# Chunk 1's triangular inverse on VectorE, behind chunk 0's, with none on GpSimd

## The chip, the cores and the metric

The kernel runs on one core of a Trainium2 chip. The metric is the device time of one execution in microseconds, the median of three runs. The engines of the core are TensorE (PE: matmuls, and PEld: loads of their stationary side), VectorE (DVE), ScalarE (ACT), GpSimd (POOL) and SyncE (SP, which issues most DMAs).

## What is computed

A delta-rule attention over 768 steps for 4 x 8 heads of width 48, then a dense layer pair with silu, then a mixture of 8 experts with top-1 routing.

```python
k_n = k / (np.linalg.norm(k, axis=-1, keepdims=True) + 1e-06)
for t in range(S):
    y[:, :, t] = np.einsum('bhd,bhde->bhe', q[:, :, t], state)
    v_old = np.einsum('bhde,bhd->bhe', state, kt)
    state = state + bt[:, :, :, None] * np.einsum('bhd,bhe->bhde', kt, vt - v_old)
h = x @ w_in;  x = (h * (1.0 / (1.0 + np.exp(-h)))) @ w_out      # 3072 x 384, inner 2048
out = x.copy(); out[do_compute] = xc + gate * (relu(xc @ w1[e]) @ w2[e])
```

## The kernel before

**Chunks.** The 768 steps are cut into 12 chunks of 64. In a chunk the recurrence becomes a triangular system for each of the 32 heads: `grams` makes the products of keys (tiles `g`, then `Gd` and `G21`), `inverse(c)` inverts the 32x32 diagonal blocks of all heads at once into the tile `Xb`, and `chain(c, b)` uses `Xb` for each of the four batches b: `ks`, `u1`, `g21u`, `u2` (tiles `ru`, `vp`, `U`, `SU`), the new state (`supd`, tile `St`) and the output of the chunk (`yout`, tiles `py` and `x`; a high part and a rest, `lo`). When the last `lo` of a chunk is there, two DMAs `x<-x` finish the tile, and the dense layers of that chunk can start: `l1(c, m)` (matmuls `hp<-x,w`) and `l2(c, m)` (`xp<-gh,w` and `xp<-gl,w`) for 16 blocks m. `x2out` then takes the sum `xp` out (`xt`), and transposes it for the router (matmuls `xr`, tile `xs`).

**The inverse.** It transposes `Gd` into `Gi`, makes the norms in 18 small instructions (tile `nw`), and then goes through 31 columns j from 31 to 1 with two instructions each, `mul` (writes `tmp`) and `sub` (writes `X`). Each depends on the one before it. `last()` scales `X` and transposes it into `Xb`. Chunk 0 works in `X`/`Gi0`; chunk 1 works in `X1` (a part of the tile `spare`) and in `Gi1`, two tiles that lie where the dense weights of blocks 13 and 14 go later, so the loads of those (`raw` of `late`) wait for chunk 1's inverse.

**Where chunk 1's inverse runs.** `E = nc.gpsimd if c == 1 else V` (line 487): all 62 column instructions of chunk 1, and two scalings of `Gi` ahead of them, are GpSimd's; the transposes, the norms and `last` are VectorE's.

**The weights.** The dense weights come as 64-bit floats. `convert` turns each of 32 blocks into a pair of fp32r tiles: ScalarE scales the high words (`w<-raw`), VectorE does one shift (TENSOR_SCALAR) and two merges (SCALAR_TENSOR_TENSOR `w<-raw,w`), ScalarE copies the high part, and GpSimd, or VectorE for 8 of the 32, subtracts it for the rest (TENSOR_TENSOR `w<-w,w`). This goes on while chunk 0's and chunk 1's chains and chunk 0's dense layers run.

**The order.** Up to chunk 1's chain the order on each engine is made when the kernel is built, by a scheduler that goes by priorities (`rank`: CHAIN, PREP, INV, CONV, MOE of a chunk) and by its own estimate of times. From chunk 2 on `period(c)` writes the order out by hand. Each engine works through its instructions strictly in that order.

Of the kernel before, what the change touches and what calls it, by code (L numbers as in the profile page):

```python
# [57 lines left out]
def kernel(  # L58
# [25 lines left out]
    nc = InOrder(tc)  # L84
# [352 lines left out]
    def inverse(c):  # L437

        steps = []
        V = nc.vector  # L440
# [43 lines left out]
        steps.append(lambda: V.tensor_tensor(out=w[4], in0=w[3], in1=bet[:, c, :], op=ALU.mult))  # L484
        steps.append(lambda: V.tensor_tensor(out=w[4], in0=w[4], in1=w[3], op=ALU.mult))

        E = nc.gpsimd if c == 1 else V
        pre = E is nc.gpsimd

        def scale(y0):  # L490
            return (nc.gpsimd if c else V).tensor_tensor(
# [4 lines left out]
        def flat(j, r0, r1):  # L496
            f = (r0 - j // 2) * j
            return tmp[:, f:f + (r1 - r0) * j].rearrange("p (n j) -> p n j", j=j)

        def mul(j, r0, r1):  # L500
# [3 lines left out]
            if pre:  # L504
                return E.tensor_tensor(out=flat(j, r0, r1), in0=a, in1=b, op=ALU.mult)
            return V.scalar_tensor_tensor(
# [3 lines left out]
        def sub(j, r0, r1):  # L510
            return E.tensor_tensor(
                out=X[:, r0:r1, 0:j], in0=X[:, r0:r1, 0:j], in1=flat(j, r0, r1), op=ALU.subtract
            )
# [565 lines left out]
    def prep():  # L1079
        while free and todo:  # L1080
            g = todo.popleft()
            c, b = g // B, g % B
            j = slots[g] = free.popleft()
            with rank(c - 1, PREP):
                if c == 0 and b == B - 1:
                    prep_0()
                elif c:
                    with rank(c - 2, PREP) if c > 1 else rank(-2, 3):
                        if c == 1:
                            clear(j)  # L1090
                            load_kt(c, b, j, nc.sync)
                        load_qk(c, b, nc.sync)
                        nc.sync.dma_start(out=PQ[j], in_=qp[c, b])
                    if c > 1:
                        prep_t(c, b)
                        if c == FIRST:
                            prep_g(c, b)
                    elif b == B - 1:
                        js1[:] = [slot(c, i) for i in range(B)]
                        grams(c, js1, 1)  # L1100
            if b == B - 1 and 0 < c < FIRST:
                with rank(0, INV):
                    last_of[c] = inverse(c)
            if b == B - 1 and not c:
                return
# [45 lines left out]
    def period(c):  # L1151


        more = c + 2 < NCH
        late = LATE if c == FIRST else 0
        inv = deque(inverse(c + 1) if c + 1 < NCH else ())
        if late:
            inv.extendleft(reversed(inverse(c)))
# [306 lines left out]
```

## Time and profile before

| what | value |
|---|---|
| median of three runs | 906.33 us (905.14 to 906.43) |
| the profiled execution | 903.69 us |
| its span, first to last instruction | 902.0 us |
| PE busy | 811.0 us, 90% |
| DVE busy | 618.6 us, 69% |
| ACT busy | 474.8 us, 53% |
| POOL busy | 367.3 us, 41% |
| mean granted clock of TensorE | 0.935 of full speed |

Times in the rows are microseconds from the span's start. The rows show one execution, the profiled one. A row of the timeline is: start, duration, engine, line, operation, what it writes `<-` what it reads, shape, how many merged; in brackets the idle time of the engine before it and what ended that. All instructions of the kernel's own work carry line 43, that of the helper that records them, so one goes by tile names.

### The profile page before, as it was taken

What the parts mean: (1) busy time and instruction counts of PE and PEld (TensorE: products, weight loads), DVE (VectorE), ACT (ScalarE), POOL (GpSimd) and SP (SyncE); (2) the same over time, 40 slices, a digit from 0 to 9 for tenths busy, and PEclk for the clock granted to TensorE, in tenths of its full rate; (3) what the DMA queues carried; (4) which work ended last, traced back from release to release, by engine and by line L of the source; (5) the groups of instructions that cost most, each with busy time, mean ns of one, the idle gap of its engine ahead of it and who ended that gap; (6) DMA issues with size and microseconds to landing.
All of it is one profiled execution on the core that took longest, in us unless ns stands there. A gap on an engine that the chain in (4) does not pass through costs nothing. (4 is left out here: it accounts for less than half of the span.)

```text
span 902.0 us, 26074 instructions
## 1 busy us (share of the span) xinstructions
PE 811.0 (90%) x10385; PEld 775.4 (86%) x10385; DVE 618.6 (69%) x1776; ACT 474.8 (53%) x1290; POOL 367.3 (41%) x533
## 2 busy tenths in 40 slices
PE   9075987797899999999999999999998968999994
PEld 9074977786799999999999999999998968999994
DVE  4998795698586877778697777779424029765731
ACT  3257875336465564746566574744455354555620
POOL 5477553151333433333342333334345452454320
PEclk7565899899899999999999999999999989999998
DMA  8963211212421414133221414211109126767300
GB/s 291 400 223 109 68 40 40 49 38 60 131 76 48 123 52 142 52 98 96 58 88 52 142 51 125 70 46 33 42 4 299 27 59 198 246 215 222 105 21 24
DMA packets 66355, 96.10 MB, mean 107 GB/s; under 512 B 10730, under 2 KB 47672, under 8 KB 66224
## 3 DMA queue, kind: packets, MB, share of 16 engines
q1 hardware_dynamic: 63408, 89.70, 32.7%
q0 software_dynamic: 2816, 4.65, 1.8%
q8 instruction: 83, 1.36, 0.7%
q14 instruction: 48, 0.39, 0.2%
HBM read 80.79 MB, written 12.91 MB: 104 GB/s over the span
## 5 line engine op out<-in xcount | busy, mean ns | idle before, releaser
L43 POOL TENSOR_TENSOR gl<-gf,gh 128x256 fp32r<-128x256 f32 x192 | 149.1, 777 | 348.2 <-ACT gf L43 304.1
L43 PE MATMUL hp<-x,w 128*128 128x256 f32 x1728 | 256.0, 293 | 8.9 <-DMA x<-x 3.9
L43 PEld LDWEIGHTS hp<-x,w 128*128 128x128 f32 x1728 | 224.2, 194 | 17.0 <-DVE xs L43 5.2
L43 PE MATMUL xp<-gh,w 128*128 128x256 f32 x1152 | 172.6, 286 | 6.9 <-ACT gh L43 6.4
L43 PEld LDWEIGHTS xp<-gh,w 128*128 128x128 f32 x1152 | 153.9, 192 | 8.1 <-ACT gh L43 7.1
L43 DVE SCALAR_TENSOR_TENSOR tmp<-X,nw,Gi 128x126 f32<-128x126 f32 (+22 forms) x341 | 139.0, 408 | 10.4
L43 ACT ACTIVATE gh<-hp 128x256 fp32r<-128x256 f32 x192 | 73.7, 384 | 135.2 <-PE hp L43 134.3
L43 DVE TENSOR_TENSOR X<-X,tmp 128x126 f32<-128x126 f32 (+22 forms) x341 | 101.9, 299 | 8.6
L43 PE MATMUL xp<-gl,w 128*128 128x256 f32 x576 | 103.5, 288 | 2.1 <-POOL gl L43 2.0
L43 PEld LDWEIGHTS xp<-gl,w 128*128 128x128 f32 x576 | 82.8, 191 | 4.2 <-POOL gl L43 3.1
L43 ACT ACTIVATE gf<-hp 128x256 f32<-128x256 f32 x192 | 72.6, 378 | 5.7 <-POOL gl L43 5.6
L43 PE MATMUL ehp<-exh,ew 128*128 128x256 f32 x384 | 66.5, 282 | 0.0
L43 ACT ACTIVATE SU<-St 32x192 f32<-32x192 f32 (+1 forms) x176 | 63.6, 361 | 2.7
L43 DVE COPY_PREDICATED PQ<-mU,g 128x512 f32<-128x512 uint8 x44 | 32.3, 738 | 46.6 <-ACT G L43 40.8
L43 ACT ACTIVATE ew<-eraw 128x768 fp32r<-128x768 f32 x64 | 53.3, 843 | 20.7 <-PE yp L43 14.8
L43 PE MATMUL g<-kq,KtB 128*128 128x128 f32 (+1 forms) x384 | 54.3, 299 | 9.8 <-DVE PQ L43 6.4
L43 DVE TENSOR_TENSOR vp<-vp,ru 64x192 f32<-64x192 f32 x92 | 31.6, 347 | 45.3 <-PE ru L43 41.4
L43 DVE TENSOR_TENSOR ew<-eraw,ew 128x768 fp32r<-128x768 f32 x48 | 49.9, 1046 | 17.7 <-ACT ew L43 17.5
L43 PEld LDWEIGHTS g<-kq,KtB 128*128 128x128 f32 x384 | 50.9, 212 | 11.0 <-DVE PQ L43 6.9
L43 PEld LDWEIGHTS ehp<-exh,ew 128*128 128x128 f32 x384 | 58.3, 190 | 0.0
L43 PE MATMUL yp<-ew,egh 128*128 128x384 f32 x256 | 57.5, 341 | 0.0
L43 POOL TENSOR_TENSOR ew<-eraw,ew 128x768 fp32r<-128x768 f32 x16 | 30.3, 1895 | 57.4 <-ACT ew L43 57.2
(144 smaller groups left out, 1276.6 us busy)
## 6 DMA issues: line engine op xcount, KB each, us to landing
eraw<-in_w_dram SPq DMA_DIRECT2D x64, 384.0 KB, 4.4
kq<-in_qk_dram SPq DMA_DIRECT2D x44, 256.0 KB, 3.9
PQ<-in_qp_dram SPq DMA_DIRECT2D x44, 256.0 KB, 4.3
ki<-in_ki_dram SPq DMA_DIRECT2D x44, 192.0 KB, 2.9
raw<-in_w_out_dram SPq DMA_DIRECT2D x16, 384.0 KB, 7.0
raw<-in_w_in_dram SPq DMA_DIRECT2D x16, 384.0 KB, 7.8
x2s<-xs SPq DMA_DIRECT2D x48, 98.5 KB, 2.3
v<-in_v_dram SPq DMA_DIRECT2D x24, 192.0 KB, 3.9
```

The lines of the kernel that those rows point to most:

```text
L43: r = f(*args, **kw)
```

## The change

Line 487 becomes `E, pre = V, False`. Chunk 1's inverse then takes the branch of the other chunks: `mul` is one SCALAR_TENSOR_TENSOR on VectorE that multiplies by the scale `w[4]` on its way, `sub` a TENSOR_TENSOR on VectorE, and the two scalings of `Gi1` fall away.

```diff
-        E = nc.gpsimd if c == 1 else V
-        pre = E is nc.gpsimd
+        E, pre = V, False
```

The scheduler then builds another order for everything up to chunk 1's chain. Three places of it follow. Names are as in the kernel; a number behind a name is its buffer: `X_122`, `tmp_126`, `Gi_121` are chunk 0's inverse, `spare`, `tmp_127`, `Gi_123` and `Gi_124` chunk 1's, `w_...` weights, which got other numbers.

VectorE, in the middle of chunk 0's inverse (column 14 and on), before:

```order
L43 SCALAR_TENSOR_TENSOR tmp_126<-X_122,nw,Gi_121 128x126
L43 TENSOR_TENSOR X_122<-X_122,tmp_126 128x9x14
L43 SCALAR_TENSOR_TENSOR tmp_126<-X_122,nw,Gi_121 128x130
L43 TENSOR_TENSOR X_122<-X_122,tmp_126 128x10x13
L43 SCALAR_TENSOR_TENSOR tmp_126<-X_122,nw,Gi_121 128x120
```

VectorE at the same place, after:

```order
L43 SCALAR_TENSOR_TENSOR tmp_126<-X_122,nw,Gi_121 128x126
L43 SCALAR_TENSOR_TENSOR tmp_127<-spare,nw,Gi_124 128x31
L43 TENSOR_TENSOR X_122<-X_122,tmp_126 128x9x14
L43 TENSOR_TENSOR spare<-spare,tmp_127 128x31
L43 SCALAR_TENSOR_TENSOR tmp_126<-X_122,nw,Gi_121 128x130
L43 SCALAR_TENSOR_TENSOR tmp_127<-spare,nw,Gi_124 128x30
L43 TENSOR_TENSOR X_122<-X_122,tmp_126 128x10x13
L43 TENSOR_TENSOR spare<-spare,tmp_127 128x30
```

From here to the end of chunk 0's inverse, 29 instructions of chunk 1's stand between chunk 0's; the other 33 stand one by one among the conversions behind it.

VectorE, where chunk 1's inverse ends (`Xb<-spare`), before:

```order
L43 SCALAR_TENSOR_TENSOR w_1019<-raw_272,w_1019 128x384
L43 TENSOR_TENSOR w_1024<-w_1019,w_1024 128x384
L43 TENSOR_TENSOR spare<-spare,nw 128x512
L43 TENSOR_SCALAR w_1034<-w_1034 128x384 x2
L43 STREAM_TRANSPOSE Xb<-spare 128x32x16
```

VectorE, the same place, after:

```order
L43 TENSOR_TENSOR spare<-spare,tmp_127 128x16
L43 SCALAR_TENSOR_TENSOR nw<-nw 128x32
L43 TENSOR_TENSOR spare<-spare,nw 128x512
L43 TENSOR_SCALAR w_1122<-w_1122 128x384
L43 TENSOR_TENSOR nw<-nw 128x32
L43 TENSOR_TENSOR w_1112<-w_1107,w_1112 128x384
L43 STREAM_TRANSPOSE Xb<-spare 128x32x16
```

`w_1024` of before is the `l2` weight of block 8, `w_1112` of after that of block 14 (the `w_1114` of before): `Xb` of chunk 1, and with it chunk 1's chain, now stands behind most of the conversions.

TensorE, where chunk 0's dense layers end and chunk 1's begin, before:

```order
L43 MATMUL xp<-gh,w_1114 128x256 x6
L43 MATMUL hp<-x,w_971 128x256 x7
L43 MATMUL xp<-gl,w_1114 128x256 x3
L43 MATMUL hp<-x,w_971 128x256 x2
L43 MATMUL xp<-gh,w_1129 128x256 x6
L43 MATMUL xp<-gl,w_1129 128x256 x3
L43 MATMUL xr<-iwg,xt 128x138 x6
L43 MATMUL hp<-x,w_986 128x256 x9
```

TensorE, the same place, after:

```order
L43 MATMUL xp<-gl,w_1127 128x256 x3
L43 MATMUL py<-PQ_115,SU_118 64x64
L43 MATMUL ru<-SU_118,ki 48x48 x8
L43 MATMUL py<-PQ_115,SU_118 64x64 x7
L43 MATMUL ru<-SU_119,ki 48x48 x8
L43 MATMUL py<-PQ_116,SU_119 64x64 x8
L43 MATMUL hp<-x,w_969 128x256 x9
L43 MATMUL xr<-iwg,xt 128x138 x6
L43 MATMUL hp<-x,w_984 128x256 x9
```

The end of chunk 1's chain (`py`) now stands behind the last matmul of chunk 0's dense layers, and nothing stands between it and chunk 1's first `hp`.

## Rows read from the trace of the kernel before

**Rows 1.** Busy us of each engine, granted clock (PEclk), DMA share, GB/s, by stage.

```profile
core 0: us, PE busy (x) PEld busy (x) DVE busy (x) ACT busy (x) POOL busy (x), PEclk, DMA share, GB/s
51.00:82.50 31.50, 22.40 (x437) 20.29 (x435) 31.02 (x61) 23.50 (x59) 27.11 (x41) 0.61 0.47 142
147.86:190.90 43.04, 32.46 (x294) 31.00 (x294) 28.91 (x92) 15.16 (x47) 11.52 (x15) 0.92 0.18 35
190.90:902.00 711.10, 673.61 (x8806) 646.12 (x8806) 469.26 (x1395) 375.73 (x1023) 264.61 (x366) 0.98 0.33 96
50.04:123.45 73.41, 58.82 (x892) 54.36 (x890) 63.07 (x122) 55.95 (x147) 50.49 (x68) 0.70 0.32 99
```

**Rows 2.** GpSimd: chunk 1's inverse begins; its busy us from 51 on.

```profile
35.48 2.16 POOL L43 TENSOR_TENSOR Gi<-Gi,nw 128x512 f32<-128x512 f32 x2 [5.84 <-DVE nw L43]
...
51.00:86.40 35.40, 21.75 (x39) 0.60 0.43 128
```

**Rows 3.** VectorE's timeline: undisturbed conversions, chunk 1's Xb, a weight's rest.

```profile
77.38 0.35 DVE L43 TENSOR_SCALAR w<-w 128x384 int32<-128x384 int32 x1
77.65 0.54 DVE L43 SCALAR_TENSOR_TENSOR w<-raw,w 128x384 int32<-128x384 int32 x1
...
86.31 0.69 DVE L43 TENSOR_TENSOR spare<-spare,nw 128x512 f32<-128x512 f32 x1 [3.83 <-POOL spare L43]
...
87.45 1.05 DVE L43 STREAM_TRANSPOSE Xb<-spare 128x512 f32<-128x512 f32 x1
...
122.26 0.36 DVE L43 TENSOR_TENSOR vp<-vp,ru 64x192 f32<-64x192 f32 x1 [1.31 <-PE ru L43]
...
123.45 1.15 DVE L43 TENSOR_TENSOR w<-w,w 128x384 fp32r<-128x384 f32 x1
```

**Rows 4.** VectorE: the last lo of chunks 0, 1, 2, and chunk 2's Xb.

```profile
78.39 0.41 DVE L43 TENSOR_TENSOR x<-py,x 128x256 fp32r<-128x256 f32 x1
...
143.86 0.42 DVE L43 TENSOR_TENSOR x<-py,x 128x256 fp32r<-128x256 f32 x1
...
186.83 1.13 DVE L43 STREAM_TRANSPOSE Xb<-X 128x512 f32<-128x512 f32 x1
...
222.15 0.41 DVE L43 TENSOR_TENSOR x<-py,x 128x256 fp32r<-128x256 f32 x1
```

**Rows 5.** TensorE: the first hp of chunks 0 and 1, the second xr.

```profile
82.50 4.18 PE L43 MATMUL hp<-x,w 128*128 128x256 f32 x18 [1.58 <-DMA x<-x]
...
147.86 1.07 PE L43 MATMUL hp<-x,w 128*128 128x256 f32 x7 [0.72 <-DMA x<-x]
...
154.72 0.97 PE L43 MATMUL xr<-iwg,xt 128*128 128x138 f32 x6 [2.36 <-ACT gf L43]
```

**Rows 6.** VectorE's timeline, the same inverse beside GpSimd's, and its end.

```profile
45.20 0.43 DVE L43 TENSOR_TENSOR X<-X,tmp 128x70 f32<-128x70 f32 x1
...
50.04 1.05 DVE L43 STREAM_TRANSPOSE Xb<-X 128x512 f32<-128x512 f32 x1
```

**Rows 7.** VectorE's timeline, chunk 0's inverse with the norms (nw) in between.

```profile
31.08 0.36 DVE L43 SCALAR_TENSOR_TENSOR tmp<-X,nw,Gi 128x133 f32<-128x133 f32 x1
31.35 0.19 DVE L43 SCALAR_TENSOR_TENSOR nw<-nw 128x32 f32<-128x32 f32 x1
31.47 0.30 DVE L43 TENSOR_TENSOR X<-X,tmp 128x133 f32<-128x133 f32 x1
31.69 0.18 DVE L43 SCALAR_TENSOR_TENSOR nw<-nw 128x32 f32<-128x32 f32 x1
```

**Rows 8.** Groups of VectorE, 50 to 82.4 us: xcount, busy us, mean ns.

```profile
L43 DVE SCALAR_TENSOR_TENSOR w<-raw,w 128x384 int32<-128x384 int32 x23 | 14.9, 679 | 0.0
L43 DVE TENSOR_SCALAR w<-w 128x384 int32<-128x384 int32 x11 | 5.6, 529 | 0.2 <-ACT w L43 0.2
```

**Rows 9.** ScalarE's timeline around the second xr.

```profile
151.04 2.96 ACT L43 ACTIVATE SU<-St 32x192 f32<-32x192 f32 x8
...
154.29 0.38 ACT L43 ACTIVATE gf<-hp 128x256 f32<-128x256 f32 x1
```

## The prediction

> **What bounds the kernel now.** I read the page first, then a table of busy time by stage, then the timelines of the engines from 30 to 230 us, and last the order that the change gives. From 190.90 us to the end TensorE is busy 673.6 of 711.1 us [rows 1], and the order there is written by hand and stays. So what the change does is done before that point, and it reaches the end one to one: a start of chunk 2's chain that comes 1 us earlier ends the kernel 1 us earlier.
>
> Before it, three things follow each other. From 51 to 82.5 us (chunk 0's chain beside the weight conversions) VectorE is busy 31.02 of 31.50 us: it is the bound, and TensorE and ScalarE are not [rows 1]. GpSimd works on chunk 1's inverse from 35.48 us on, and VectorE stands idle 3.83 us for it until 86.31 [rows 2, 3]. Then chunk 0's dense layers go as the conversions let them, with chunk 1's chain between them, until chunk 1's x is there: its last `lo` ends at 144.28, and its first `hp` starts at 147.86, having waited 0.72 us for the DMA `x<-x` [rows 4, 5]. From 147.86 to 190.90 TensorE works 32.46 of 43.04 us [rows 1]; chunk 2's inverse on VectorE sets the pace, and its loop can go on only when the second `xr` (154.72) has been taken out. So I follow the second `xr`: where it lands, the rest lands.
>
> **What the change adds, removes and moves.** The sum goes along VectorE up to `Xb` of chunk 1, then along the chain.
>
> Chunk 0's `Xb`: it starts at 50.04 [rows 6]. After the change the stretch from 35.3 on holds 27 instructions of chunk 0's inverse and 29 of chunk 1's, in turn. Two chains in turn hide each other's latency: where norms stand between, the next instruction starts 0.27 us after a product of 133 elements, 0.22 after a subtraction of 133 and 0.12 after one of 32 [rows 7]. With sizes from 16 to 136 I take 0.20 as the mean: 56 x 0.20 = 11.2. Three conversion steps (a shift takes 0.27 from start to start, a merge, 0.54 long, some 0.47) [rows 3] and the scaling (0.69 long [rows 3], some 0.6) make 13.0: 35.6 + 13.0 = 48.6, 1.4 us earlier. That one chain took 14.7 us before is GpSimd's doing: beside it a subtraction of 70 elements lasted 0.43 us, one of 133 alone 0.30 [rows 6, 7]. If the two chains did not overlap at all it would be 52 to 54, 2 to 4 later.
>
> Chunk 1's `Xb`: in the new order it stands right behind the rest of `l2`'s block 14, which in the trace comes at 123.45. From 50.04 to there VectorE was busy 63.07 of 73.41 us [rows 1, 3]. To these 73.4 us come the other 33 instructions of the inverse, 33 x 0.20 = 6.7. Off go nine instructions of chunk 1's chain, now behind (`vp` is 0.36 long, `x` 0.41, less what overlaps: 0.3 each, 2.6) [rows 3, 4], the wait of 3.83 for GpSimd and one of 1.31 for that chain [rows 3]. And off goes what GpSimd's inverse took from VectorE. Undisturbed, a merge lasts 0.54 us and a shift 0.35 [rows 3]; from 50 to 82.4 their means were 0.679 and 0.529 [rows 8], so 23 x 0.14 + 11 x 0.18 = 5.2 us were lost beside 27.1 us of GpSimd work [rows 1], 0.19 per us. The column instructions lost a little more [rows 6], and I take 0.25: of 21.75 us of GpSimd's inverse [rows 2] 5.4 us. Together 73.4 + 6.7 - 2.6 - 5.1 - 5.4 = 67.0, less 0.4 since `Xb` (1.05 long, some 0.9) now comes behind that place and the rest (some 0.5) in front of it: 48.6 + 66.6 = 115 us, against 87.45 [rows 3]. The loss per us of GpSimd could be 0 (its other work moves up and collides in its place) or 0.4: 121 or 112.
>
> Chunk 1's chain: from `Xb` to the end of the last `lo` chunk 0 took 50.04 to 78.80, 28.8 us, with all four batches side by side; chunk 2, in two halves with dense blocks between, took 186.83 to 222.56, 35.7 us [rows 4, 6]. Chunk 1's own 87.45 to 144.28 [rows 3, 4] is no guide: over fifty conversion instructions of VectorE stood between, and now seventeen do. It goes in two halves like chunk 2, but with fewer dense blocks between, so 31, with 28.8 and 35.7 as ends: the last `lo` ends at 146 (140.8 to 157).
>
> From there: 3.6 us for the DMA (78.80 to 82.50 and 144.28 to 147.86) [rows 4, 5], so the first `hp` is at 149.6, 1.8 us later than before; 1.4 to 2.1 us for the nine matmuls (seven took 1.07 at 147.86, eighteen 4.18 at 82.50) [rows 5], and 0.9 for `gh` and `gf` (0.38 each [rows 9]), which free the buffer of the second `xr`. It would start at 152.3. Before, it started at 154.72, since ScalarE first made eight copies `SU<-St` of 2.96 us and then `gh` and `gf` [rows 5, 9]; in the new order these copies stand ahead, between the `x` of the chain. So the late `hp` is more than paid for: 152.3 - 154.72 = **-2.4 us**.
>
> The rest costs nothing that I can find. GpSimd loses 30 us of work and nobody waits for what is left. The load of block 13's weights waits for the last product of the inverse, some 3 us ahead of `Xb`, and is wanted about 7 us later. The conversions end some 13 us behind chunk 1's `Xb`, by 130, and chunk 0's last dense block needs them until about 140: in front of the chain's end at 146.
>
> The profiled execution has 902.0 us from first to last instruction and 903.69 in all, 2.64 less than the median of 906.33. The difference of -2.4 goes on the median: **903.9 us**.
>
> **A rule against the change.** From 51 to 82.5 us VectorE has 0.48 us to spare and gets more work [rows 1]. The Trainium skill (Perfetto Trace Analysis, Optimizing Scalar/DVE Operations) says that with VectorE saturated work may be moved to ScalarE or even GpSimd, though it warns that VectorE and GpSimd share a read port. By the first half this change goes the wrong way, and `Xb` of chunk 1 would be at 121; by the warning most of what is added comes back.
>
> **The rivals.**
>
> *Slower: chunk 1's chain comes too late behind the conversions.* Break-even is a last `lo` at 148.4: `Xb` at 115 and a chain of 33.4, or a chain of 31 and `Xb` at 117.4. For it: VectorE was full, ScalarE works 56 of 73.4 us in the same stretch [rows 1] and must turn every conversion round, and chunk 2's chain took 35.7 us. With 117 and 35.7 the second `xr` is at 159, +4.3: 910.6 us; with 121 it is +8, 914.6. Against it: the relief that the rows show.
>
> *No change.* The copies that kept `gf` at ScalarE come back at the same place in another form (the copies now stand between the last two `x`, and can delay the last `lo` by 2 to 3 us instead), or a chain of 33 us: within 1.8 us of 906.3. That the change does not do what it says is excluded by the order: no column instruction is left on GpSimd.
>
> *Much faster: a GpSimd instruction stops VectorE for as long as it lasts.* With 0.5 us lost per us of GpSimd, twice what I take, the relief is 10.9 instead of 5.4, and the second `xr` is 5.5 earlier still: 898.4 us. The rows say 0.19 to 0.25, so it has little weight. This is what the Trainium skill (SBUF — State Buffer, Who interferes with whom) makes likely: a VectorE instruction with two SBUF inputs contends with a GpSimd one that reads SBUF, and whoever issues first holds the port pair for the whole instruction. The trace agrees in kind (merges of 0.679 against 0.54 us), not in full size.
>
> **How the numbers follow.** Chances: forecast (gain of 1.8 to 6 us) 0.41, much faster 0.06, no change 0.25, slower 0.28. A measurement of this kernel can tell about 0.2%, 1.8 us, from no change: faster 0.47, same 0.25, slower 0.28. The range takes in the much faster case down to 899.5 and the slower one up to 911; left out are the ends where 121 and 35.7, or 112 and 28.8, come together.
>
> **What would show it.** Right: VectorE's steps between 36 and 48 us of 0.2 us and `Xb` at 48 to 49; chunk 1's `Xb` at 112 to 119 without a wait for GpSimd; merges from 50 to 82 us nearer to 0.54; the first `hp` of chunk 1 at 148 to 151 after an idle TensorE of 5 us, and the second `xr` about 2 us behind it. Wrong: merges as slow as before; a last `lo` later than 148.4; waits of VectorE for ScalarE's `w` that add up to more than 5 us from 50 to 115; TensorE's granted clock staying near the 0.61 of 51 to 82.5 us [rows 1] while chunk 1's chain runs, so that each matmul step of the chain is longer.

## The result: slower by 1.1%

The kernel after takes 916.23 us (median of 4 runs, 914.65 to 917.9), the kernel before on the same chip 906.38 (4 runs, 905.14 to 906.82): a ratio of 1.0113 with a 95% interval of 1.0095 to 1.0132. The forecast was 903.9 us, the range 899.5 to 911. What came is the prediction's rival "Slower: chunk 1's chain comes too late behind the conversions", at its far corner (914.6 us there).

The head of the page of the kernel after, and under it VectorE's timeline of the places of [rows 3, 4, 6]:

```profile
span 914.9 us, 26069 instructions
...
PE 814.0 (89%) x10385; PEld 778.4 (85%) x10385; DVE 622.1 (68%) x1838; ACT 474.3 (52%) x1290; POOL 339.9 (37%) x469
```

```profile
49.42 1.05 DVE L43 STREAM_TRANSPOSE Xb<-X 128x512 f32<-128x512 f32 x1
...
122.39 1.12 DVE L43 STREAM_TRANSPOSE Xb<-spare 128x512 f32<-128x512 f32 x1
...
149.53 0.63 DVE L43 TENSOR_TENSOR vp<-vp,ru 64x192 f32<-64x192 f32 x2 [6.08 <-PE ru L43]
...
156.66 0.42 DVE L43 TENSOR_TENSOR x<-py,x 128x256 fp32r<-128x256 f32 x1 [1.63 <-ACT x L43]
165.21 0.19 DVE L43 TENSOR_REDUCE xs<-xr 128x10 f32<-128x30 f32 x1 [8.12 <-ACT xs L43]
```

VectorE works only 3.5 us more than before (622.1 against 618.6 us), and nobody works much longer. What has changed is when things happen. Chunk 0's `Xb` comes at 49.42 (forecast 48.6, before 50.04), chunk 1's at 122.39 instead of 87.45, and chunk 1's last `lo` ends at 157.1 instead of 144.3. VectorE has nothing to do for 8.12 us after that. TensorE's timeline, to be held against [rows 5], says why:

```profile
161.01 2.26 PE L43 MATMUL hp<-x,w 128*128 128x256 f32 x9 [5.15 <-DMA x<-x]
163.07 2.49 PE L43 MATMUL xr<-iwg,xt 128*128 128x138 f32 x12
```

TensorE itself stands still for 5.15 us until chunk 1's `x` is complete. The second `xr` (the seventh of these twelve) starts at 164.45, 9.7 us later than before [rows 5]; the median is 9.85 us later. So the delay of that point did reach the end one to one, as the prediction had it, only with the other sign.

The table of busy time by stage (columns as in [rows 1]), for the kernel after:

```profile
36.00:50.00 14.00, 3.35 (x32) 3.32 (x33) 14.00 (x62) 1.51 (x3) 1.08 (x1) 0.50 1.03 402
50.00:82.40 32.40, 21.67 (x443) 19.74 (x441) 31.94 (x72) 23.92 (x62) 10.10 (x10) 0.66 0.51 157
82.40:122.40 40.00, 29.71 (x197) 27.60 (x197) 37.41 (x79) 25.12 (x65) 23.23 (x21) 0.88 0.11 30
49.42:122.40 72.98, 51.96 (x643) 47.92 (x642) 69.92 (x151) 49.03 (x127) 33.33 (x30) 0.78 0.30 90
```

and for the kernel before, in the same stretches:

```profile
50.00:82.40 32.40, 23.40 (x446) 21.27 (x444) 31.90 (x62) 23.50 (x59) 27.01 (x41) 0.61 0.49 150
82.40:122.40 40.00, 34.41 (x437) 32.09 (x438) 30.16 (x60) 31.75 (x87) 22.44 (x26) 0.76 0.20 61
```

Only up to 82.4 us does GpSimd (the fifth engine of a row) have less to do, 10.10 us instead of 27.01. From there to chunk 1's `Xb` it works as long as before, 23.23 against 22.44 us, while VectorE goes from 30.16 to 37.41. TensorE loses 4.7 us of work in that second stretch: chunk 1's chain, which stood between chunk 0's dense blocks, is missing there and comes later; some five to seven of chunk 0's dense blocks are still there beside it, and beside its last 4.6 us (from 152.48) none.

### The profile page after: what moved, and what is told of

Its sections match the earlier page's. It is cut to its first block, busy times and chain, and to the rows that moved or that the text cites. A ratio compares the mean times of both kernels' runs of the same rounds, so it can differ in the third digit from the quotient of the medians.

```text
span 914.9 us, 26069 instructions
## 1 busy us (share of the span) xinstructions
PE 814.0 (89%) x10385; PEld 778.4 (85%) x10385; DVE 622.1 (68%) x1838; ACT 474.3 (52%) x1290; POOL 339.9 (37%) x469
## 5 line engine op out<-in xcount | busy, mean ns | idle before, releaser
L43 PE MATMUL hp<-x,w 128*128 128x256 f32 x1728 | 258.0, 294 | 18.2 <-DMA x<-x 7.2
L43 DVE SCALAR_TENSOR_TENSOR tmp<-X,nw,Gi 128x126 f32<-128x126 f32 (+22 forms) x341 | 135.3, 397 | 10.0
L43 PE MATMUL ehp<-exh,ew 128*128 128x256 f32 x384 | 66.6, 283 | 0.0
L43 ACT ACTIVATE ew<-eraw 128x768 fp32r<-128x768 f32 x64 | 53.3, 843 | 20.4 <-PE yp L43 14.7
```

Of the source, the lines that this page charges most:

```text
L43: r = f(*args, **kw)
```

## The experiments

Theory **place**: the loss is that chunk 1's `Xb` stands behind nearly all conversions, so that its chain ends after everything else. Theory **load**: the 62 added instructions cost VectorE these 10 us wherever they stand. Beside it stands the question where the relief went that the prediction expected of GpSimd. Each time is to be held against the runs of the kernel before on its own chip, so ratios are given.

**e1: the same work, another place.** Each conversion step is tied to one more of the last 33 instructions of chunk 1's inverse, and what is left to the last of them.

```diff
-            with tc.issue_after(gates.popleft() if gates else done):
+            with tc.issue_after(gates.popleft() if gates else tail):
...
+    n = 0.0
+    for i in pace["inv", 1][48:]:
+        n += 1.0
+        while n >= 1:
+            gates.append(i.ins)
+            n -= 1
+    tail = pace["inv", 1][-1].ins
```

> The kernel after, with each conversion step of VectorE behind the second one tied to one more of the last 33 column instructions of chunk 1's inverse, so that the inverse gets every second place on VectorE instead of every third or fourth; the work is the same. In the new order chunk 1's Xb has 43 rows fewer in front of it (row 245 instead of 288). Theory 'place' (the loss of 9.9 us comes from chunk 1's Xb standing behind nearly all conversions, 122.4 us instead of 87.5, so that its chain ends after everything else): Xb of chunk 1 at 92 to 100 us, the last lo of chunk 1 back at 143 to 149, time 904 to 909 us. Theory 'load' (VectorE is full up to that point and the 62 added column instructions cost their 10 us wherever they stand): the conversions end 8 to 10 us later than in the kernel before, chunk 0's last dense block and chunk 1's chain with them, time 913 to 917 us.

Measured: 906.96 us (10 runs) against 905.4 (22 runs), ratio 1.002, 1.0003 to 1.0037. VectorE's and TensorE's timelines:

```profile
88.99 1.12 DVE L43 STREAM_TRANSPOSE Xb<-spare 128x512 f32<-128x512 f32 x1
...
133.90 0.41 DVE L43 TENSOR_TENSOR x<-py,x 128x256 fp32r<-128x256 f32 x1
...
138.65 1.95 DVE L43 SCALAR_TENSOR_TENSOR w<-raw,w 128x384 int32<-128x384 int32 x4
```

```profile
152.92 0.97 PE L43 MATMUL xr<-iwg,xt 128*128 128x138 f32 x6 [2.36 <-ACT gf L43]
```

All columns are still VectorE's, yet eight of the ten microseconds are back. `Xb` is at 88.99, the last `lo` ends at 134.3, ten microseconds ahead of the kernel before, and the conversions end behind it, at 140.6. The second `xr` is held by ScalarE as in [rows 5, 9]. `Xb` and `lo` came earlier than place had expected, but its time was hit. The ten microseconds at the `lo` brought nothing, because another path is now the later one: chunk 0's last dense matmul ends at 148.79 (before 150.59), and the second `xr` starts 4.1 us behind that in both.

**e5: the same place, without the work.** The kernel before, with GpSimd's inverse; only the last three instructions of it wait.

```diff
+            seen["rest", m, z] = (nc.vector if z and m % 2 == 0 else nc.gpsimd).tensor_tensor(
...
-    with rank(0, INV):
+    with rank(0, INV), tc.issue_after(seen["rest", 14, 1].ins):
         last_of.pop(1)()
```

> The kernel before, GpSimd's inverse and all, with one wait more: the last three instructions of chunk 1's inverse (nat, the scaling and Xb) wait for VectorE's rest of l2's block 14, the instruction behind which they stand in the kernel after. VectorE gets no instruction more than in the kernel before. Theory 'place': the loss comes back without the added work; Xb of chunk 1 at 112 to 122 us, the last lo 33 to 36 us behind it, time 909 to 916 us. Theory 'load' (62 more instructions on VectorE make the loss): 905 to 907 us.

Measured: 914.12 us (4 runs) against 905.65 (17 runs), ratio 1.0082, 1.0056 to 1.0108. VectorE's timeline, its waits from 82.4 to 123 us (us in total, times, the longest), the busy time there, and TensorE's timeline:

```profile
122.98 1.07 DVE L43 STREAM_TRANSPOSE Xb<-spare 128x512 f32<-128x512 f32 x1
...
155.00 0.42 DVE L43 TENSOR_TENSOR x<-py,x 128x256 fp32r<-128x256 f32 x1 [1.63 <-ACT x L43]
```

```profile
DVE w L43 <- ACT w L43: 6.5, 3, 4.5
DVE PQ L43 <- ACT G L43: 3.0, 1, 3.0
```

```profile
82.40:122.40 40.00, 31.55 (x213) 29.42 (x213) 30.78 (x58) 26.49 (x69) 26.56 (x30) 0.84 0.12 37
```

```profile
158.93 2.26 PE L43 MATMUL hp<-x,w 128*128 128x256 f32 x9 [4.73 <-DMA x<-x]
160.99 2.76 PE L43 MATMUL xr<-iwg,xt 128*128 128x138 f32 x12
```

`Xb` is a microsecond later than place had expected and the last `lo` follows it by 32.4 us (33 to 36 expected), but the time was hit. VectorE is idle for 9.2 of these 40 us, and the kernel is slow all the same; the end has the shape of the kernel after, with TensorE 4.73 us idle in front of the first `hp`. e1 and e5 together settle it: **the place makes the loss** (0.82% by it alone), and the added work a small part (0.2% in e1, 0.37% by the upper end of its interval; 0.3% between e5 and the kernel after, whose intervals overlap).

**e3: GpSimd's load put back.** The kernel after, with the column instructions made by GpSimd too, on a copy (`bal_x`).

```diff
         for j in range(31, 0, -1):
             for f in (mul, sub):
                 steps.append(lambda f=f, j=j, r0=r0: f(j, r0, 16))
+                if c == 1:
+                    steps.append(lambda k=f is sub, j=j, r0=r0: dum(j, r0, k))
```

> The kernel after, and beside it GpSimd makes the 62 column instructions and the two scalings of chunk 1 as well, on a copy that nobody reads: GpSimd has the load of the kernel before, VectorE that of the kernel after, and nobody waits for the copy. The prediction's step of 5.4 us of relief: if GpSimd's inverse took 0.25 us of VectorE's time per us, chunk 1's Xb comes 5.4 us later than in the kernel after (at 128 us) and the time is 921 to 922 us. Theory 'no relief' (the rests that GpSimd still makes collide in the inverse's place, as much as before): Xb within 1.5 us of 122.4, time 915 to 918 us.

Measured: 921.05 us (4 runs) against 905.4, ratio 1.0172, 1.0138 to 1.0206; 0.6% over the kernel after. VectorE's timeline and the busy time by stage:

```profile
53.63 1.05 DVE L43 STREAM_TRANSPOSE Xb<-X 128x512 f32<-128x512 f32 x1
...
125.69 1.07 DVE L43 STREAM_TRANSPOSE Xb<-spare 128x512 f32<-128x512 f32 x1
```

```profile
36.00:50.00 14.00, 0.00 (x0) 0.00 (x0) 14.00 (x49) 1.51 (x3) 11.66 (x26) 0.50 1.03 401
50.00:82.40 32.40, 24.22 (x458) 22.43 (x458) 32.09 (x68) 18.85 (x49) 25.62 (x44) 0.61 0.41 136
```

The time looks like the relief that the prediction had counted, but it is not where the prediction put it. Chunk 0's `Xb` comes 4.2 us later: from 36 to 50 us VectorE gets 49 instructions through instead of 62 beside 11.66 us of GpSimd's. From there to chunk 1's `Xb` it is 72.1 us, against 73.0 in the kernel after. That stretch of e3 holds a merge, a shift, a rest and a column subtraction less, 2.1 us by the start-to-start times of the kernel after. So in the stretch of the conversions 16.1 us more of GpSimd's work (49.4 against 33.3) cost VectorE about 1 us, an estimate of 0.07 per us, where the prediction had 0.25. `Xb`, 3.3 us later than in the kernel after, lies between the two expectations.

**e4: no inverse for chunk 1 at all.** The kernel before without 56 of GpSimd's 62 column instructions.

```diff
         for j in range(31, 0, -1):
+            if pre and 1 < j < 31 and j != 28:
+                continue
```

> The kernel before with 56 of the 62 column instructions of chunk 1's inverse left out (the first, the last and one of the middle are kept, on GpSimd), so that neither engine makes them: what is computed for chunk 1 is not the inverse. Measures what the inverse on GpSimd costs the kernel before at all, wait and contention together. With relief (0.25 us per us of GpSimd work): the wait of 3.83 us and 5 to 6 us of VectorE time are gone, chunk 1's last lo ends 6 to 9 us earlier, time 897 to 900 us. Without relief: the wait alone, 902 to 905 us. If the chain of chunk 1 is bound by the dense blocks and ScalarE anyway: 905 to 907 us, and then no place or engine for this inverse can gain anything.

Measured: 899.55 us (7 runs) against 905.4, ratio 0.9945, 0.9918 to 0.9971.

```profile
65.27 1.08 DVE L43 STREAM_TRANSPOSE Xb<-spare 128x512 f32<-128x512 f32 x1
...
126.61 0.35 DVE L43 TENSOR_TENSOR x<-py,x 128x256 fp32r<-128x256 f32 x1
```

With the inverse for nothing, chunk 1's last `lo` is 17 us earlier than in [rows 4], and the kernel gains 5.9 us. The time is the one expected with relief, but the `lo` moved twice as far as expected there, so it is no sign of relief. That is an estimate of what any arrangement of this inverse could bring with the rest left alone. Against the prediction's idea that every microsecond counts from there on: seventeen at the last `lo` became 8.0 at the second `xr` (146.70) and six at the end. The 8.0 are those of chunk 0's last dense matmul, which ends at 142.57 instead of 150.59: where the chain is early, the second `xr` follows the end of these blocks, by 4.1 us in the kernel before, e1, e2 and e4.

**e6: without GpSimd's subtractions of the weights.** The kernel after, the dense layers taking the high half in place of the rest.

```diff
-            (nc.vector if z and m % 2 == 0 else nc.gpsimd).tensor_tensor(
-                out=lo, in0=w, in1=hi.bitcast(F32), op=ALU.subtract
-            )
+            if z and m % 2 == 0:
+                nc.vector.tensor_tensor(out=lo, in0=w, in1=hi.bitcast(F32), op=ALU.subtract)
+            else:
+                one.add((m, z))
```

> The kernel after with GpSimd's subtractions w<-w,w (the low halves of the weights, 23 of 1.0 us or more up to 140 us) left out; the dense layers take the high half in their place, so the result is less exact. Measures what stretches VectorE's instructions in the kernel after. If it is these subtractions of GpSimd: from 50 us to chunk 1's Xb the merges w<-raw,w fall from 0.595 to 0.48 us from start to start, the products tmp from 0.39 to 0.27 and the subtractions spare from 0.29 to 0.21, and Xb of chunk 1 comes at 106 to 112 us instead of 122.4. If it is something else (latency of the dependent column instructions, ScalarE, DMA writes): means within 0.03 us of those of the kernel after and Xb at 119 to 123 us.

Measured in a single execution: chunk 0's `Xb` at 47.22, chunk 1's at 113.38, a stretch of 66.2 instead of 73.0 us. VectorE's groups there (xcount, busy us, mean ns), first of e6, then of the kernel after:

```profile
L43 DVE SCALAR_TENSOR_TENSOR w<-raw,w 128x384 int32<-128x384 int32 x53 | 29.4, 576 | 0.1
L43 DVE TENSOR_SCALAR w<-w 128x384 int32<-128x384 int32 x28 | 9.4, 352 | 0.2
L43 DVE SCALAR_TENSOR_TENSOR tmp<-spare,nw,Gi 128x136 f32<-128x136 f32 (+16 forms) x17 | 6.2, 363 | 0.0
L43 DVE TENSOR_TENSOR spare<-spare,tmp 128x136 f32<-128x136 f32 (+16 forms) x17 | 5.3, 311 | 0.0
```

```profile
L43 DVE SCALAR_TENSOR_TENSOR w<-raw,w 128x384 int32<-128x384 int32 x47 | 30.1, 666 | 0.1
L43 DVE TENSOR_SCALAR w<-w 128x384 int32<-128x384 int32 x24 | 10.4, 452 | 0.2
L43 DVE SCALAR_TENSOR_TENSOR tmp<-spare,nw,Gi 128x136 f32<-128x136 f32 (+16 forms) x17 | 7.6, 449 | 0.0
L43 DVE TENSOR_TENSOR spare<-spare,tmp 128x136 f32<-128x136 f32 (+16 forms) x17 | 5.8, 341 | 0.0
```

Merges fall from 0.666 to 0.576 us, shifts from 0.452 to 0.352. Undisturbed a shift is as long (0.35), a merge 0.54 [rows 3]. This stretch of e6 holds six merges and four shifts more than that of the kernel after (4.2 us by e6's start-to-start times), so like for like some 11 us are gone. So most of what stretches the conversions after the change are GpSimd's subtractions of the weights, which the change doesn't touch. It is not all of it: `Xb` came 1.4 us later than the bound, and the column instructions were expected to fall further, to 0.27 and 0.21 from start to start, and got to 0.30 and 0.27. What holds those was not looked into.

**e7: fewer dense blocks beside the chain.** The kernel after, without six of chunk 0's sixteen `l1` (9 to 14) and seven `l2` (8 to 14).

```diff
-            if m:
+            if m and (c, m - 1) in mm:
...
     for m in range(MF + 1):
-        moe_part(0, m)
+        if not 9 <= m <= MF - 2:
+            moe_part(0, m)
```

> The kernel after with about half of chunk 0's dense blocks left out (hidden blocks from 9 to the last but one), so that chunk 0's output lacks them; chunk 1's Xb keeps its place behind the conversions. Tells what makes chunk 1's chain 34.7 us long. If it is the dense blocks that TensorE and ScalarE have to do in between: 28 to 31 us from Xb to the end of the last lo. If it is the two halves one behind the other and ScalarE's copies: 33 to 35 us.

Measured in a single execution, VectorE's timeline:

```profile
120.84 1.07 DVE L43 STREAM_TRANSPOSE Xb<-spare 128x512 f32<-128x512 f32 x1
...
152.56 0.42 DVE L43 TENSOR_TENSOR x<-py,x 128x256 fp32r<-128x256 f32 x1 [1.04 <-ACT x L43]
```

From `Xb` to the last `lo` 32.1 us, between the two expectations (28 to 31, 33 to 35) and 2.6 less than the 34.7 of the kernel after. But the run changes TensorE's clock too. The busy time by stage (columns as in [rows 1]) over the chain, of e7 and then of the kernel after:

```profile
120.80:153.00 32.20, 22.63 (x402) 19.55 (x402) 21.93 (x55) 21.17 (x56) 8.09 (x9) 0.55 0.19 57
```

```profile
122.40:157.10 34.70, 27.88 (x497) 24.68 (x495) 22.59 (x55) 24.02 (x66) 14.92 (x15) 0.93 0.17 50
```

With fewer matmuls the granted clock over the chain was 0.55, near the lower level of 1.2 GHz, instead of 0.93, and sixteen matmuls `ru<-vp,Xb` took 0.85 us instead of 0.53. So the 2.6 us are what the missing blocks gave less what the lower clock took, and the price of the blocks stays open. In e5, with as late an `Xb`, nearly as many blocks and a clock of 0.80, the chain took 32.4 us.

**e2: half and half.** VectorE makes columns 31 to 16, which fit beside chunk 0's inverse, GpSimd 15 to 1.

```diff
-        E, pre = V, False
+        K = 16 if c == 1 else 0
...
-            if pre:
-                return E.tensor_tensor(out=flat(j, r0, r1), in0=a, in1=b, op=ALU.mult)
+            if j < K:
+                return nc.gpsimd.tensor_tensor(out=flat(j, r0, r1), in0=a, in1=b, op=ALU.mult)
```

> Half of the change: of chunk 1's inverse VectorE makes columns 31 to 16 (32 instructions, which fall beside chunk 0's inverse) and GpSimd columns 15 to 1 (30 instructions and one scaling). Theory 'place': Xb of chunk 1 at 78 to 86 us without a wait of VectorE for GpSimd, the rest as in the kernel before or a little earlier, time 901 to 906 us. Theory 'load': what is added lies in the latency of chunk 0's inverse, and GpSimd has some 15 us less to do: 899 to 904 us. If neither the wait for GpSimd nor its load mattered in the kernel before: 905 to 908 us.

Measured: 903.47 us (10 runs) against 905.4 (22 runs), ratio 0.998, 0.9958 to 1.0002. `Xb` of chunk 1 at 84.40 after a wait of 0.75 us for GpSimd, the last `lo` ends at 136.2, the second `xr` starts at 149.82 (before 154.72). Both theories had allowed for this time; it tells them apart no further. Chunk 0's last dense matmul ends at 145.69, 4.9 us earlier than before, like the second `xr`. Whether the half alone gains is not quite settled.

**e8, e9, e10: the seam to chunk 2.** In e2 VectorE waits 5.83 us for TensorE ahead of the copy `xt`, and ScalarE's eight copies `SU<-St` still stand in front of the second `xr`. Two moves, on e2 (e8, e9) and on the kernel before (e10):

```diff
-            step(26)
+            step(44)
             x2a(c - 2)
             for i in range(2):
                 load_v(c, i, nc.sync)
                 load_k(c, i, nc.sync)
-                pre_s(c, i, SU[i])
...
             if i == 0:
                 finish(c - 2, 0)
+                if late:
+                    for b in A:
+                        pre_s(c, b, SU[b])
```

> The half and half kernel with two moves at the seam to chunk 2: the eight copies SU<-St of 2.96 us stand behind the two xr instead of ahead of them, and 44 instead of 26 instructions of chunk 2's inverse stand ahead of VectorE's copy xt, which waits 5.8 us for TensorE. If the second xr, held by these copies, and chunk 2's inverse set the time from there on (as the prediction says): second xr 2.5 us earlier, chunk 2's Xb 2.5 to 6 us earlier than 182.8, time 897 to 901 us. If chunk 0's last dense block sets it: 902 to 904 us, as without the two moves.

> The half and half kernel with two moves at the seam to chunk 2: the eight copies SU<-St of 2.96 us behind the two xr instead of ahead of them, and 44 instead of 26 instructions of chunk 2's inverse ahead of VectorE's copy xt, which waits 5.8 us for TensorE (with a limit that keeps chunk 3's instructions from being drawn forward with them). If the prediction's premise holds that the second xr and chunk 2's inverse set the pace from 150 to 190 us: second xr 2 us and chunk 2's Xb some 6 us or more earlier than 182.8, time 897 to 900 us. If TensorE's work and chunk 3's preparation behind it set it: chunk 2's Xb earlier, but chunk 3's Xb within 1 us of 226.4, time 902 to 904.5 us.

> The two moves at the seam alone, on the kernel before (GpSimd makes chunk 1's inverse). If the second xr and chunk 2's inverse set the pace there: 2 to 6 us faster than the kernel before, 900 to 904 us. If not: 904.5 to 907 us, and what the half and half kernel gains is the half alone.

e8 drew chunk 3's first instructions forward too, ahead of the data that they read (`Gi<-Gd` at 171.47, `Gd<-g` at 172.54), so chunk 3's inverse there is another one; 903.7 us (12 runs) against 905.65, ratio 0.997, 0.9952 to 0.9988. e9 has the limit that its expectation names: **897.0 us** (12 runs) against 901.86 (23 runs), ratio 0.9951, 0.9932 to 0.9969, faster than both kernels. e10: 900.54 us (12 runs) against the same, ratio 0.9979, 0.9962 to 0.9996. On this chip the kernel before takes 3.5 us less than on the one of e2, so the 897.0 hits its expectation (897 to 900) by the chip alone; taken as a ratio (some 901 us there) it lies between the two that were written down. The 1.3 us of e10 fall short of its 2 to 6. `Xb` of chunks 2 and 3 on VectorE's timeline, in e2 and then in e9:

```profile
182.78 1.08 DVE L43 STREAM_TRANSPOSE Xb<-X 128x512 f32<-128x512 f32 x1
...
226.42 1.09 DVE L43 STREAM_TRANSPOSE Xb<-X 128x512 f32<-128x512 f32 x1
```

```profile
169.77 1.04 DVE L43 STREAM_TRANSPOSE Xb<-X 128x512 f32<-128x512 f32 x1
...
221.85 1.06 DVE L43 STREAM_TRANSPOSE Xb<-X 128x512 f32<-128x512 f32 x1
```

The second `xr` is 1.2 us earlier than in e2, chunk 2's inverse 13.0 us, chunk 3's 4.6, and the ratio 0.3% lower. That chunk 2's inverse sets the pace, the prediction's premise for the stretch up to 190.90 us, holds for a delay but for a gain only as far as the next bound, chunk 3's preparation and TensorE's blocks (which of the two, no run shows). In e8 chunk 3's `Xb`, at 225.69, gave nearly all of it back.

## Why the prediction was wrong

**Right.** Chunk 0's `Xb` (48.6 forecast, 49.42 measured; steps of 0.2 us between 36 and 48 us); 0.5 of the 0.8 us were there at 34 us, before the two orders differ. In e4, with 5.2 instead of 11.8 us of GpSimd beside it, chunk 0's inverse alone took 13.0 us from the product of column 14 to `Xb` instead of 14.7; in the kernel after both inverses in turn took 13.6, so the 29 added instructions cost next to nothing there. No instruction of VectorE up to chunk 1's `Xb` waits for GpSimd any more. The DMA `x<-x` (3.6 forecast, 3.9 from 157.1 to 161.0). That a delay of the second `xr` reaches the end one to one. And the mechanism of the slower rival with its break-even: a last `lo` later than 148.4 loses.

**Wrong: the sum up to chunk 1's `Xb`**, 66.6 us forecast from chunk 0's `Xb` and 73.0 measured. The measured column is worked out from the start-to-start times of all of VectorE's instructions in the stretches of both kernels; the relief is what is left over.

| term | forecast | measured |
|---|---|---|
| stretch of the kernel before, to chunk 1's new place | 73.0 | 73.6 |
| column instructions, 33 | +6.7 | +10.8 |
| chunk 1's chain, now behind | -2.6 | -2.5 |
| waits that vanish | -5.1 | -7.4 |
| relief from GpSimd's inverse, on all the rest | -5.4 | -1.5 |
| sum | 66.6 | 73.0 |

The waits gave 2.3 us more than reckoned. Two terms failed: the price of a column instruction (4.1 us) and the relief from GpSimd's inverse (3.9 us).

*The column instructions.* The price of 0.20 us came from [rows 7], two chains in turn with GpSimd at rest. Among conversions each took 0.33: 16 products 0.39 and 17 subtractions with one scaling 0.29 from start to start, together 11.4, less the 0.6 of the scaling that the kernel before had too. With GpSimd's subtractions gone (e6) it is 0.30 and 0.27, so they explain less than half of the 4.1 us; the rest is open.

*The relief.* The step reckoned a loss per microsecond of GpSimd work over a stretch where short column instructions and long subtractions were mixed, and gave back that rate for the column instructions alone. GpSimd's groups from 50 to 82.4 us (xcount, busy us, mean ns), first of the kernel before, then of after:

```profile
L43 POOL TENSOR_TENSOR spare<-spare,tmp 128x120 f32<-128x120 f32 (+14 forms) x17 | 10.1, 596 | 0.9
L43 POOL TENSOR_TENSOR tmp<-spare,Gi 128x126 f32<-128x126 f32 (+14 forms) x16 | 10.1, 633 | 1.1
L43 POOL TENSOR_TENSOR w<-w,w 128x384 fp32r<-128x384 f32 x5 | 5.5, 1098 | 2.2 <-ACT w L43 2.2
```

```profile
L43 POOL TENSOR_TENSOR w<-w,w 128x384 fp32r<-128x384 f32 x7 | 9.9, 1420 | 21.7 <-ACT w L43 21.7
```

With 20.2 us of column instructions gone, seven subtractions of 1.42 us on the mean were left where there had been five of 1.10 (one of the seven lasted 2.97 us, the others 1.16 on the mean), and the merges of VectorE went from 0.679 us [rows 8] only to 0.640:

```profile
L43 DVE SCALAR_TENSOR_TENSOR w<-raw,w 128x384 int32<-128x384 int32 x21 | 12.8, 640 | 0.1
```

From 82.4 us on there was next to nothing to relieve. e3 gives the same small price from the other side, 0.07 us per us. The upper bound that the prediction gave this term, "its other work moves up and collides in its place", is what happened; with it alone `Xb` would have been forecast at 121. The rule of the Trainium skill that the prediction had weighed against the change (Perfetto Trace Analysis, Optimizing Scalar/DVE Operations), that a full VectorE may be helped by moving some of its work away, pointed in the direction that the result took, but in e1 the load itself made 0.2%.

**Wrong: the chain**, 31 us forecast and 34.7 measured. It was taken nearer to chunk 0's 28.8 than to chunk 2's 35.7 because fewer dense blocks stand between. They were fewer, but not by much: 48 matmuls `hp` and 63 `xp` stood between, against 62 and 72 in chunk 2's. What they cost the chain stays open, since e7 changed the clock with them.

**A small one behind it.** The second `xr` came 7.4 us after the last `lo`, not 6.1. The DMA took 0.3 us more, and TensorE's granted clock explains most of the rest: in the row of 161 to 165.5 us, after 5 us of idling, it was 0.56, near the lower level of 1.2 GHz, and the nine `hp` took 2.26 us, where nine take 1.24 in a stretch of full clock in e2 (132 to 147 us) and the forecast had some 1.8; behind them the six matmuls of the first `xr` took 1.4 us, where six take 0.8 at 240 us at full clock.

```profile
161.00:165.50 4.50, 4.49 (x22) 4.40 (x22) 0.19 (x1) 1.15 (x3) 0.72 (x1) 0.56 0.00 0
```

Together 0.8 (chunk 0's `Xb`) + 6.4 + 3.7 + 1.3 = 12.2 us, and the result is 12.3 us over the forecast. The range failed because it left out the case in which both upper ends, 121 and 35.7, come together. That a late `Xb` by itself makes the chain long is not shown: in e5 `Xb` was as late and the chain 32.4 us.

## What to carry to other kernels

When a dependent series of instructions moves to a busy engine, ask first where the scheduler will put its last one: at a low rate between ready work it ends when that work ends, and the chain behind it is then alone. Holding the ready work back by a few waits took back eight of the ten microseconds here (e1); moving only as much as fits into another series' latency (e2), with the next seam mended too (e9), got ahead of the kernel before. And a rate of interference read from a mixture of short and long instructions belongs to neither of them: ask what the other engine will be doing instead.

## What the runs showed of the hardware

GpSimd's short column instructions (0.45 to 0.65 us) and its long subtractions (most of them 1.0 to 1.5 us) do not cost VectorE the same. Some 16 us of the short ones more, among conversions, cost about 1 us (e3). With the subtractions left out (e6) GpSimd worked 18.2 us less in the stretch from chunk 0's `Xb` to chunk 1's (15.1 against 33.3), and some 11 us were gone like for like: 0.6 per microsecond, an estimate. But beside two dependent chains of small instructions the short ones cost 4.2 us for some 12 (e3, 36 to 54 us). Whether VectorE slows GpSimd in turn was not tried: three of GpSimd's subtractions lasted 2.0 to 3.2 us in the kernel after and none so long in the kernel before. The Trainium skill (SBUF — State Buffer, Who interferes with whom) has whoever issues first hold the shared port pair for the whole instruction. That the long ones cost more per microsecond goes with it, but no run here separates the port from other causes.

Single executions of one kernel lie a few microseconds apart (the kernel before 902.26 to 909.06 on one chip), and not evenly: behind the `xr` at about 490 us the profiled execution of the kernel before needs 409.0 us, e1's 413.9 and e2's 412.5 for the same instructions. Positions in the first quarter differ as well: e10 has the order of the kernel before on VectorE up to 140 us, and there the same instructions start 1.2 us earlier from 31 us on and 2.4 us earlier at 140. So a difference of one or two microseconds between positions of two traces shows nothing by itself; lengths within one trace agree better (from the same product of chunk 0's inverse to `Xb` 14.71 and 14.67 us). e1 is 1.9 us ahead of the kernel before at that `xr`, 1.3 of which were there at 34 us, and 0.2% behind by the timed runs. Where in the experts' part this comes from is open.
